# One-hot rows by wide transpositions and small transfers in the start of a routed attention and SwiGLU kernel

## The chip, the cores and the metric

The kernel runs on one core of one Trainium2 chip. The metric is the device time of one execution in microseconds (us), the median of several runs. The core has five engines that work side by side and meet only at semaphores: TensorE (PE, with weight loads shown apart as PEld), VectorE (DVE), ScalarE (ACT), GpSimd (POOL) and SyncE (SP, which here only issues transfers). Each engine runs its own instructions in the order in which they were written.

## The reference

Attention in which a query sees only the keys of its own cluster, then a SwiGLU feed-forward layer without biases. There are 4 batches, 8 heads, 768 positions, 64 columns a head, 16 clusters a head; the layer has width 512 and inner width 1536.

```python
q_assign = np.argmax(np.einsum('bhsd,hcd->bhsc', q_n, c_n), axis=-1)
k_assign = np.argmax(np.einsum('bhsd,hcd->bhsc', k_n, c_n), axis=-1)
mask = q_assign[:, :, :, None] == k_assign[:, :, None, :]
scores = np.where(mask, scale * np.matmul(q, k.transpose(0, 1, 3, 2)), -1e9)
attn = exp(scores - max); attn = attn / sum(attn)
x = np.matmul(attn, v)                      # then (tokens, 512)
xn = x / sqrt(mean(x * x) + 1e-6) * rms_g
out = (silu(xn @ w_gate) * (xn @ w_val)) @ w_out
```

## The kernel before, in words

**The mask as sixteen more rows.** For each head the transposed queries and keys are kept in bf16 tiles `qext` and `kext`, 80 rows high: 64 rows of the head and below them 16 rows that hold, for each position, a one-hot of its cluster. The matmul over 80 rows (L349, `s`) then gives the score plus a large constant where the clusters agree, and the exponential on ACT (L353, `pT`) takes the constant off again, so that pairs of different clusters vanish. Everything below about `kext` and `qext` is about filling these two parts in time: the 64 rows by casts (L241), the 16 rows by the one-hot path.

**Units and steps.** A unit is half of a batch's queries (384 positions) with all 8 heads. A head of a unit is three steps; each step is two score matmuls (L349) into one of two PSUM buffers and one exponential of 128 x 768 (L353). `attention` writes the steps out in order and puts other work between them. I number the 24 steps of the first unit 0 to 23; head h has steps 3h to 3h + 2. The steps after them belong to the second unit. After the middle step of each head it issues `pv` of the head before: 18 matmuls (L367, `acc`) that multiply the exponentials with the values. Two heads share one `acc` tile, and there is only one buffer for it (`ps_a`); after the odd head DVE takes the reciprocal of the sums (L372, `inv`) and scales (L374, `x`), which frees the buffer for the next two heads. So pv of heads 2, 4 and 6 waits for an x. This pv is written right after a step's scores, and the next step's scores stand behind it on PE.

**The first unit has no feed-forward work to fill it.** From the second unit on, matmuls of the feed-forward layer for the unit before stand between the scores. The first unit's gaps instead hold the preparation of the eight heads of batch 0, written out by hand in `first`, a table from step to function, with `gap1` and `gap5` for steps 1 and 5. Steps that have no entry get one warming matmul (`more`, L133); those with `None` get nothing.

**Preparation of a head.** Queries and keys are loaded by SP, turned by PE in three 128 x 128 transposes (`trans`, L222, tile `tq` in PSUM), and copied to `qkT` by ACT (L228) or by DVE (L226). POOL casts `qkT` into `kext` and `qext` (`casts`, L241); a head needs its two halves of keys (K0, K1) and the first half of queries (Q0) for the first unit, and Q1 for the second. POOL also casts the values (`vcast`, L244) and issues the loads of the gate and value weights (`load_gv`, L205). Group 0 is heads 0 to 3, group 1 heads 4 to 7; `trans(1, h, m)` is head 4 + h, keys for m = 1, queries for m = 0. `late` is the same for the first heads of batch 1.

**The one-hot path before.** `pair_clusters(p)` serves heads 2p and 2p + 1: PE multiplies `qkT` with the centroids (L321, `sc`), then DVE transposes (L324), takes the largest of 16 (L327) and compares (L328), which writes zeros and ones into `pads[p]`: 128 partitions, 32 for each of two heads and queries or keys. `head(n)` then calls `under` twice: one DVE transposition of 32 x 384 (L333) writes the keys' 16 rows, and the padding below them, straight into `kext`, another the queries' into `qext`. The rows go through DVE in 32-bit words that hold two bf16 values.

**Order before.** Step 1: pair_clusters(1), then heads 4 to 7's preparation begins, head(2), head(3). Step 5: pair_clusters(2), head(4). Step 7: head(5). Step 9: pair_clusters(3). Step 10: head(6). Step 13: DVE casts head 6's keys itself, then head(7). Step 14 issues second_batch, loads for batch 1, behind `hold`, a small transfer by SP that waits for an inv. At the second unit's step 5 the first unit's normalized tokens are transposed (L429), and then the first gate matmul (L450) runs. `norm` before it is a chain on DVE: squares (L392), a root (L403, L145 to L154), scaling (L414).

Of the kernel before, what the change touches and what calls it, by code (L numbers as in the profile page):

```python
# [10 lines left out]
BF16 = mybir.dt.bfloat16  # L11
I32 = mybir.dt.int32
# [10 lines left out]
def kernel(  # L23
# [12 lines left out]
    nc = tc.nc  # L36
    B, H, S, D = q.shape
    NC = centroids.shape[1]
# [6 lines left out]
    HG = 4  # L45
# [52 lines left out]
    def load_qk(n):  # L98
        if n < B * H:
            load(n, 0)  # L100
            load(n, 1)
# [22 lines left out]
    qext = [const.tile([P, HG, S], BF16, name=f"qext{i}") for i in range(4)]  # L124
    kext = [const.tile([P, HG, S], BF16, name=f"kext{i}") for i in range(4)]
# [76 lines left out]
    def load_gv(i):  # L202
        c = slice(i * DF // 2, (i + 1) * DF // 2)
        for w, of in ((wg, moe_w_gate), (wv, moe_w_val)):
            nc.gpsimd.dma_start(out=w[:, :, c], in_=of[:, c].rearrange("(c p) f -> p c f", p=P))  # L205
# [7 lines left out]
    def trans(g, h, part, on=None):  # L213
        if (g, h // 2) not in qkT:
            qkT[g, h // 2] = qk32.tile([P, 2, 2, UQ], F32, tag="qkT", name="qkT")
        qk = staged[g * HG + h]
        if g * HG + h >= BH:
            nc.vector.transpose(qkT[g, h // 2][:, h % 2, part], qk[:, part].rearrange("p t d -> p (t d)"))  # L218
            return
        ps = ps_g.tile([P, UQ], F32, tag="gen", name="tq")  # L220
        for i in range(HT):
            nc.tensor.transpose(ps[:, i * P:(i + 1) * P], qk[:, part, 2 * i:2 * i + 2].rearrange("p t d -> p (t d)"),  # L222
                                ident_f)
        to, by = qkT[g, h // 2][:, h % 2, part], 1.0 / ZS if part and g < BG else 1.0
        if on is nc.vector:
            nc.vector.tensor_scalar_mul(to, ps, by)  # L226
        else:
            nc.scalar.activation(to, ps, ACT.Copy, scale=by)  # L228
# [5 lines left out]
    def cast(on, g, h, part, es=(0, 1)):  # L234
        for e in es:
            to = cols((kext if part else qext)[g % 4][:D, h], g, e)
            of = qkT[g, h // 2][e * D:(e + 1) * D, h % 2, part]
            if on is nc.scalar:
                nc.scalar.copy(to, of)
            else:  # L240
                on.tensor_copy(to, of)  # L241

    def vcast(n):
        nc.gpsimd.tensor_copy(vbf[n // HG % 4][:, n % HG, :, :D], stagedv[n])  # L244
# [48 lines left out]
    def place(on, g, m, es=(0, 1)):  # L293

        ext = (kext if m else qext)[g % 4]
        for h in range(HG):
# [7 lines left out]
    pads = [(xp if p == 0 else outp).tile([P, NB, 32, 2], BF16, tag="o_sb" if p else "gvT", name=f"pads{p}")  # L304
            for p in range(H // 2)]
# [3 lines left out]
    def slot(n, m):  # L309

        return 32 * (2 * (n % 2) + m if n < 2 else 2 * m + n % 2)

    def pair_clusters(p, heads=(0, 1)):
        g, h = divmod(2 * p, HG)
        what = [(h + i, m) for i in heads for m in range(2)]
        at = [slot(2 * p + i, m) for i in heads for m in range(2)]
        r = slice(min(at), max(at) + 32)
        pool, tag = (ps_g, "gen") if p else (ps_s, "s") if 0 in heads else (ps_a, "acc")
        ps = pool.tile([P, 512], F32, tag=tag, name="sc")
        for a, (hh, m) in sorted(zip(at, what)):  # L320
            nc.tensor.matmul(ps[a:a + 32, :UQ], lhsT=cblk[:, g * HG + hh], rhs=qkT[g, hh // 2][:, hh % 2, m],  # L321
                             start=True, stop=True)
        sct = asg.tile([P, UQ], F32, tag="scT", name="scT", bufs=2)
        nc.vector.transpose(sct[r], ps[r, :UQ])  # L324
        cl = sct[r].rearrange("p (b e c) -> p b e c", e=2, c=NC)
        mx = ps[r, UQ:UQ + 2 * NB].rearrange("p (b e) -> p b e", e=2)
        nc.vector.tensor_reduce(mx, cl, axis=AX, op=ALU.max)  # L327
        nc.vector.tensor_tensor(pads[p][r, :, :NC].rearrange("p b c e -> p b e c"), cl,  # L328
                                mx.unsqueeze(3).broadcast_to([mx.shape[0], NB, 2, NC]), op=ALU.is_equal)

    def under(n, m):
        i = slot(n, m)
        nc.vector.transpose((kext if m else qext)[n // HG][D:D + 32, n % HG].bitcast(I32),  # L333
                            pads[n // 2][i:i + 32].rearrange("p b c e -> p (b c e)").bitcast(I32))
# [239 lines left out]
    def tokens(g, h, on=None):  # L574
        trans(g, h, 1, on)
        trans(g, h, 0, on)

    def head(n):
        under(n, 1)
        under(n, 0)  # L580

    def casts(on, n, *what):
        for m, e in what:
            cast(on, n // HG, n % HG, m, (e,))

    K0, K1, Q0, Q1 = (1, 0), (1, 1), (0, 0), (0, 1)
    pool_ = nc.gpsimd
# [31 lines left out]
    def more():  # L619
        busy(1, False)  # L620
# [3 lines left out]
    def second_batch():  # L624
        nc.sync.dma_start(out=hold, in_=invs[0].rearrange("p a t -> p (a t)"))
        for n in range(H + HG, H + NQ):
            load_qk(n)
        for n in range(H, H + AV):
            load_v(n)
        nc.sync.dma_start(out=grow, in_=moe_rms_g.unsqueeze(0).broadcast_to([P, DM]))  # L630

    def gap1():
        pair_clusters(1)
        tokens(1, 1)
        casts(pool_, 2, Q1)
        casts(pool_, 3, Q1)
        vcast(2)
        vcast(3)
        head(2)
        head(3)  # L640
        casts(pool_, 4, K0, K1, Q0)
        load_gv(0)
        casts(pool_, 5, K0, K1, Q0)

    def gap5():
        pair_clusters(2)
        casts(pool_, 6, Q0)
        vcast(4)
        casts(pool_, 7, Q0)
        for n in (4, 5):  # L650
            casts(pool_, n, Q1)
        vcast(5)
        casts(pool_, 7, K0, K1)
        vcast(6)
        vcast(7)
        for n in (6, 7):
            casts(pool_, n, Q1)
        load_gv(1)
        head(4)

    early = [lambda h=h, m=m: trans(1, h, m) for h in (2, 3) for m in (1, 0)]
    late = [lambda h=h, m=m: trans(2, h, m, nc.vector if h < 3 else None) for h in range(HG) for m in (1, 0)]
    first = {0: lambda: trans(1, 0, 0), 1: gap1, 2: early[0], 3: early[1], 4: lambda: (early[2](), early[3]()), 5: gap5,
             7: lambda: head(5), 9: lambda: pair_clusters(3), 10: lambda: head(6),
             13: lambda: (casts(nc.vector, 6, K0, K1), head(7)), 14: lambda: (more(), second_batch())}
    first.update({16: None, 19: None, 22: None})
    first.update({i: f for i, f in zip((15, 17, 18, 20, 21, 23), late)})


    due = []  # L670
# [22 lines left out]
    for u in range(1, NU):  # L693
        ffn, o, g = ffn_work(u - 1), out_work(u - 2) if u > 1 else [], u + 2
        if u == 1:
            ffn[:2] = [(2 * 0.64, lambda: gv_first(0)), (0.0, lambda: None)]
            t, c, a = group_work(2)
            t3, c3, a3 = group_work(3)
            n = LEAD - 4
            w3 = weave(t3[n:], c3)  # L700
            prep = c + a + w3[:4] + [(0.0, lambda: load_o(8))] + w3[4:] + a3[:5]
            idle = const.tile([P, 1], BF16)

            def norm():
                rms(0)
                nc.gpsimd.tensor_copy(idle, xn[0][:, CC - 1, HT - 1, P - 1:])
                for h in range(HG):
                    casts(pool_, H + h, K0, Q0, K1, Q1)

            hooks = {(1, 0, 0): late[6], (1, 0, 1): lambda: (late[7](), norm())}  # L710
            hooks.update({(1, *divmod(2 + i, HT)): t3[i][1] for i in range(n)})
            hooks[1, *divmod(LEAD - 1, HT)] = lambda: xtrans_all(0)
            fill = spread(ffn[:CUT], prep)
            attention([(1, h) for h in range(H)], fill, LEAD, hooks)
        else:
            fill = ffn_work(u - 2)[CUT:]
            fill = fill[:1] + spread(fill[1:], [(0.0, f) for _, f in (a3[5:] if u == 2 else rest)])
            fill.append((0.0, lambda u=u: rms(u - 1)))
            rows, clusters = group(g)
            fill += [(0.0, lambda n=n: load_qk(n)) for n in LATE.get(u, ())]  # L720
            n, m = {2: (8, 4), 3: (12, 4)}.get(u, (len(rows), len(clusters)))
            fill += spread(o, rows[:n]) + spread(ffn[:CUT], [(0.0, f) for _, f in rows[n:]] + clusters[:m])
            rest = clusters[m:]
            attention([(u, h) for h in range(H)], fill, 1 if g < NG else 0, ahead=1)
# [42 lines left out]
```

The softmax here doesn't subtract the row's maximum and nothing guards it: scores larger than these inputs give would overflow.

## Time and profile before

| | |
|---|---|
| time, median of 3 runs | 325.4 us (325.24 to 325.67) |
| span of the profiled execution | 323.6 us |
| PE busy | 317.5 us, 98% |
| ACT busy | 245.0 us, 76% |
| DVE busy | 217.7 us, 67% |
| POOL busy | 134.0 us, 41% |
| exponential of one step (L353) | 904 ns, 192 of them |
| cast to kext or qext by POOL (L241) | 540 and 532 ns |
| transposition of 128 x 384 by DVE (L218) | 552 ns |

A line of the page names line of code, engine, operation, output and input, and then either the start and length of one merged stretch or count, sum and mean. "Idle before" names what released the engine. A busy PE is not PE at its peak, since the ends of matmuls are modelled, and shares over the whole span hide that the stages differ: the first 40 us, in which the first unit runs without feed-forward work, have another limit than the rest.

### The profile page before, as it was taken

How to read it: one execution, taken by the hardware profiler on the slowest of the kernel's cores; microseconds unless marked ns; L12 is line 12 of the kernel's file. 1: busy time of each engine (PE TensorE's matmuls, PEld its weight loads, DVE VectorE, ACT ScalarE, POOL GpSimd, SP SyncE). 2: the span in 40 equal slices, each digit the busy share in tenths (PEclk: the TensorE clock that was granted, in tenths of full speed). 3: DMA queues.
4: the chain of work that ended last, by engine and by line, in shares of the span. 5: the costliest groups of instructions: out<-in, count | busy, mean ns of one | idle time of the engine just before them, and what ended most of it. 6: DMA issues, size and time to landing. Idle time of an engine off the chain costs nothing.

```text
span 323.6 us, 7771 instructions
## 1 busy us (share of the span) xinstructions
PE 317.5 (98%) x2847; PEld 190.4 (59%) x2847; DVE 217.7 (67%) x502; ACT 245.0 (76%) x422; POOL 134.0 (41%) x275
## 2 busy tenths in 40 slices
PE   8999999999999999999999999999999999999996
PEld 4546656565656656565566655665566656654654
DVE  6999879888586857779677685876265645681430
ACT  5999988986869877787679867897879868862322
POOL 5998198978933585046917156440000000000000
PEclk9999999999999999999999999999999999999999
DMA  7999985998445664565456440000500040004002
GB/s 254 339 234 219 200 212 100 176 172 186 80 72 118 154 130 74 117 134 139 82 93 133 134 115 34 9 18 1 149 0 2 2 113 34 0 2 138 11 1 98
DMA packets 91639, 34.64 MB, mean 107 GB/s; under 512 B 75600, under 2 KB 88528, under 8 KB 91600
## 3 DMA queue, kind: packets, MB, share of 16 engines
q1 hardware_dynamic: 84544, 27.84, 36.7%
q0 software_dynamic: 6768, 5.90, 10.3%
q8 instruction: 22, 0.36, 0.5%
q10 hardware_dynamic: 288, 0.39, 0.4%
q14 instruction: 17, 0.14, 0.1%
HBM read 28.61 MB, written 6.29 MB: 108 GB/s over the span
## 4 chain that ended last, share of the span: by engine, by line
PE 86%; ACT 4%; POOL 4%; DVE 3%; issue 1%; DMA 1%; ACTq 0%; DVEq 0%; POOLq 0%
PE gate L450 19%; PE val L450 19%; PE o L488 18%; PE s L349 17%; PE acc L367 9%; ACT pT L353 3%; PE sc L255 3%; POOL kext L241 2%; POOL qext L241 1%; DMA boot<-in_centroids_dram 1%; PE o L499 1%; POOL vbf L244 1%; ACT qkT L228 1%; DVE kext L333 1%; DVE qext L333 1%
## 5 line engine op out<-in xcount | busy, mean ns | idle before, releaser
L353 ACT ACTIVATE pT<-s,off 128x768 bf16<-128x768 f32 x192 | 170.9, 904 | 29.1 <-PE s L349 28.3
L349 PE MATMUL s<-qext,kext 80*128 80x384 bf16 x384 | 94.8, 327 | 1.2 <-ACT pT L353 0.6
L450 PE MATMUL gate<-xnT,wg 128*128 128x384 bf16 x384 | 78.6, 325 | 0.1
L450 PE MATMUL val<-xnT,wv 128*128 128x384 bf16 x384 | 78.4, 326 | 0.0
L488 PE MATMUL o<-wo,gvT 128*128 128x512 bf16 x276 | 67.7, 378 | 0.0
L472 DVE SCALAR_TENSOR_TENSOR th<-th,gate 128x384 f32<-128x384 f32 x81 | 44.5, 549 | 34.1 <-ACT th L471 33.7
L349 PEld LDWEIGHTS <-kext 80*128 80x128 bf16 x384 | 36.3, 98 | 35.0 <-issue 7.6
L476 DVE SCALAR_TENSOR_TENSOR gvT<-th,val 128x384 bf16<-128x384 f32 x81 | 44.4, 548 | 8.5 <-PE val L450 2.9
L450 PEld LDWEIGHTS <-wg 128*128 128x128 bf16 x384 | 36.2, 97 | 23.4 <-issue 0.3
L471 ACT ACTIVATE th<-gate 128x384 f32<-128x384 f32 x81 | 39.7, 490 | 12.6 <-PE gate L450 11.8
L367 PEld LDWEIGHTS <-pT 128*128 128x128 bf16 x1152 | 43.4, 97 | 9.8 <-DVE x L374 0.8
L450 PEld LDWEIGHTS <-wv 128*128 128x128 bf16 x384 | 35.7, 97 | 22.4 <-issue 0.4
L367 PE MATMUL acc<-vbf,pT 128*128 128x65 bf16 x1152 | 45.6, 193 | 0.5 <-DVE x L374 0.2
L488 PEld LDWEIGHTS <-gvT 128*128 128x128 bf16 x276 | 25.9, 97 | 26.1 <-issue 0.2
L241 POOL CAST qext<-qkT 64x384 bf16<-64x384 f32 x64 | 33.7, 532 | 17.1 <-DVE qkT L218 9.6
L298 POOL DMA_DIRECT2D qext<-oh x48 | 23.1, 492 | 34.9 <-DVE oh L287 34.9
L241 POOL CAST kext<-qkT 64x384 bf16<-64x384 f32 x60 | 32.4, 540 | 5.1 <-DVE qkT L226 2.4
L298 POOL DMA_DIRECT2D kext<-oh x48 | 23.1, 488 | 13.6 <-DVE oh L287 12.5
L491 ACT COPY o_sb<-o 128x512 f32<-128x512 f32 x23 | 13.5, 585 | 17.6 <-PE o L488 17.6
L372 DVE RECIPROCAL inv<-acc 128x6 f32<-128x6 f32 x32 | 6.0, 188 | 24.9 <-PE acc L367 24.4
L218 DVE STREAM_TRANSPOSE qkT<-qk 128x384 f32<-128x384 f32 x38 | 19.5, 552 | 0.0
L374 DVE TENSOR_TENSOR x<-acc,inv 128x384 f32<-128x384 f32 x32 | 17.8, 557 | 1.1
(80 smaller groups left out, 220.6 us busy)
## 6 DMA issues: line engine op xcount, KB each, us to landing
vs<-in_v_dram SPq DMA_DIRECT2D x32, 192.0 KB, 4.1
out_dram<-o_sb SPq DMA_DIRECT2D x23, 256.0 KB, 2.5
qk<-in_q_dram SPq DMA_DIRECT2D x76, 48.0 KB, 2.7
qk<-in_k_dram SPq DMA_DIRECT2D x76, 48.0 KB, 2.5
qk<-in_q_dram SPq DMA_DIRECT2D x13, 192.0 KB, 4.8
qk<-in_k_dram SPq DMA_DIRECT2D x11, 192.0 KB, 4.9
wg<-in_moe_w_gate_dram POOLq DMA_DIRECT2D x2, 768.0 KB, 7.9
wv<-in_moe_w_val_dram POOLq DMA_DIRECT2D x2, 768.0 KB, 11.8
```

The lines of the kernel that those rows point to most:

```text
L218: nc.vector.transpose(qkT[g, h // 2][:, h % 2, part], qk[:, part].rearrange("p t d -> p (t d)"))
L241: on.tensor_copy(to, of)
L298: on.dma_start(out=ext[D:D + NC, h, e * UQ:(e + 1) * UQ], in_=put[g, m][32 * h + e * NC:32 * h + (e + 1) * NC])
L349: nc.tensor.matmul(ps[:, j, :w] if nt == HT else flat[:, j * w:(j + 1) * w], lhsT=cols(kext[g % 4][:KR, hh], g, kc // HT, kc % HT * P, (kc ...
L353: nc.scalar.activation(pT[u, h][:, n * i:n * i + n, :w], of, ACT.Exp, bias=off, scale=scale if g >= BG else scale * ZS)
L367: nc.tensor.matmul(acc[:, h % 2, t], lhsT=pT[u, h][:, kc, t * P:(t + 1) * P], rhs=vbf[g % 4][:, hh, kc % HT * 2 + kc // HT], start=kc == 0 ...
L374: nc.vector.tensor_tensor(dst, acc[:, :, :nt, :D], inv[:, :, :nt].unsqueeze(3).broadcast_to([P, 2, nt, D]), op=ALU.mult)
L450: nc.tensor.matmul(ps, lhsT=(wv if val else wg)[:, c, f * P:(f + 1) * P], rhs=xnT[u][:, c], start=c == 0, stop=c == CC - 1)
L471: nc.scalar.activation(th, ps, ACT.Tanh, scale=0.5)
L472: nc.vector.scalar_tensor_tensor(th, th, 1.0, ps, op0=ALU.add, op1=ALU.mult)
L476: nc.vector.scalar_tensor_tensor(gvT[u][:, f, :n], gates[u], 0.5, ps, op0=ALU.mult, op1=ALU.mult)
L488: nc.tensor.matmul(outs[u], lhsT=gvT[u][:, f, t * P:(t + 1) * P], rhs=wo[:, f], start=f == 0, stop=f == FC - 1)
```

## The change

It shortens DVE's and ACT's work in the first unit. For heads 5, 6 and 7 the narrow transpositions into `kext` and `qext` go. In their place one transposition of all 128 partitions of `pads[p]` (`send`) writes the rows to the `scT` tile that pair_clusters has just finished with, and small transfers on SP's queue, two for each head, carry 16 rows each to their place: two for head 5, four for heads 6 and 7. pair_clusters(3) moves from step 9 to step 7 so that the transfers start early. Head 6's key casts go from DVE to POOL, whose list is put into a new order, and vcast(4) moves ahead of the weight load. Three copies from PSUM (L228 by ACT) become L226 by DVE: head 5's queries at step 1, head 7's queries at step 4, and one of the late ones. The late transposes start one step earlier, at step 14.

```diff
+        rows[p] = sct.bitcast(I32)
+
+    rows = {}
+
+    def send(p, heads):
+
+        nc.vector.transpose(rows[p], pads[p].rearrange("p b c e -> p (b c e)").bitcast(I32))
+        for n in heads:
+            for m in (1, 0):
+                i = slot(n, m)
+                nc.sync.dma_start(out=(kext if m else qext)[n // HG][D:D + NC, n % HG], in_=rows[p][i:i + NC].bitcast(BF16))
...
     def gap1():
+        trans(1, 1, 0, nc.vector)
         pair_clusters(1)
-        tokens(1, 1)
+        trans(1, 1, 1)
         casts(pool_, 2, Q1)
         casts(pool_, 3, Q1)
         vcast(2)
...
         casts(pool_, 4, K0, K1, Q0)
+        casts(pool_, 5, K0, K1)
+        vcast(4)
         load_gv(0)
-        casts(pool_, 5, K0, K1, Q0)
+        casts(pool_, 5, Q0)
 
     def gap5():
         pair_clusters(2)
         casts(pool_, 6, Q0)
-        vcast(4)
+        vcast(5)
+        casts(pool_, 6, K0, K1)
         casts(pool_, 7, Q0)
-        for n in (4, 5):
-            casts(pool_, n, Q1)
-        vcast(5)
+        casts(pool_, 4, Q1)
+        vcast(6)
         casts(pool_, 7, K0, K1)
-        vcast(6)
+        casts(pool_, 5, Q1)
         vcast(7)
         for n in (6, 7):
             casts(pool_, n, Q1)
         load_gv(1)
         head(4)
-
-    early = [lambda h=h, m=m: trans(1, h, m) for h in (2, 3) for m in (1, 0)]
-    late = [lambda h=h, m=m: trans(2, h, m, nc.vector if h < 3 else None) for h in range(HG) for m in (1, 0)]
+        send(2, (5,))
+
+    def gap7():
+        pair_clusters(3)
+        send(3, (6, 7))
+
+    early = [lambda h=h, m=m: trans(1, h, m, nc.vector if (h, m) == (3, 0) else None) for h in (2, 3) for m in (1, 0)]
+    late = [lambda h=h, m=m: trans(2, h, m, nc.vector if (h, m) != (HG - 1, 0) else None) for h in range(HG) for m in (1, 0)]
     first = {0: lambda: trans(1, 0, 0), 1: gap1, 2: early[0], 3: early[1], 4: lambda: (early[2](), early[3]()), 5: gap5,
-             7: lambda: head(5), 9: lambda: pair_clusters(3), 10: lambda: head(6),
-             13: lambda: (casts(nc.vector, 6, K0, K1), head(7)), 14: lambda: (more(), second_batch())}
+             7: gap7, 14: lambda: (late[0](), second_batch())}
     first.update({16: None, 19: None, 22: None})
-    first.update({i: f for i, f in zip((15, 17, 18, 20, 21, 23), late)})
+    first.update({i: f for i, f in zip((15, 17, 18, 20, 21, 23), late[1:])})
...
-            hooks = {(1, 0, 0): late[6], (1, 0, 1): lambda: (late[7](), norm())}
+            hooks = {(1, 0, 0): late[7], (1, 0, 1): norm}
```

Steps 9, 10 and 13, which lose their entries, get a warming matmul each; step 14 loses its own.

## The prediction

> **What bounds the kernel now.** I read the slices of the page first, then the chain that ended last, then the busy time by stretch, then the timeline of each engine between 10 and 41 us. From 40 us on TensorE (PE) is at 9 tenths in every slice and the chain is nothing but PE. All the edits act before that, so the question is when the first gate matmul starts, at 40.21 us before; what moves it should move the end by as much, since the PE-bound stretch behind it keeps its work.
>
> Busy time by stretch (PE, weight loads, DVE, ACT, POOL; count of instructions in brackets):
>
> ```profile
> 17.80:22.20 4.40, 4.12 (x51) 1.96 (x48) 3.97 (x9) 4.17 (x7) 4.22 (x8) 1.00 0.91 225
> 22.20:28.20 6.00, 5.62 (x73) 3.42 (x70) 5.58 (x11) 5.75 (x8) 5.71 (x11) 1.00 1.07 188
> 28.20:34.50 6.30, 6.12 (x85) 4.75 (x84) 6.12 (x17) 6.30 (x8) 3.38 (x6) 1.00 1.11 206
> 34.50:40.20 5.70, 5.16 (x55) 3.76 (x54) 4.67 (x22) 5.38 (x10) 0.68 (x3) 1.00 1.28 214
> ```
>
> No one engine is far ahead: DVE and ACT are both near full until 34.5 us, POOL until 28. So the order of work on DVE decides as much as its sum. The chain says where it decides (start, length, what):
>
> ```profile
> 19.87 0.57 DVE kext L333
> 20.46 0.57 DVE qext L333
> 21.06 0.21 DVE inv L372
> 21.29 0.56 DVE x L374
> 21.88 0.57 DVE kext L333
> 22.48 0.57 DVE qext L333
> 23.08 0.59 DVE scT L324
> ...
> 26.47 0.57 DVE x L374
> 27.08 0.72 PE acc L367 x18
> ```
>
> Seven microseconds of the chain are DVE, and it leaves DVE at an x (L374), the instruction that frees the one accumulator bank. The timeline shows the same at the x before it:
>
> ```profile
> 21.29 0.56 DVE L374 TENSOR_TENSOR x<-acc,inv 128x384 f32<-128x384 f32 x1
> ...
> 21.93 0.71 PE L367 MATMUL acc<-vbf,pT 128*128 128x65 bf16 x18
> 22.13 2.58 ACT L353 ACTIVATE pT<-s,off 128x768 bf16<-128x768 f32 x3 [0.23 <-PE s L349]
> ...
> 22.48 0.51 PE L349 MATMUL s<-qext,kext 80*128 80x384 bf16 x2
> ...
> 28.19 6.46 ACT L353 ACTIVATE pT<-s,off 128x768 bf16<-128x768 f32 x8 [0.25 <-PE s L349]
> ```
>
> x ends at 21.85, PE starts head 2's acc matmuls at 21.93, and step 11's scores (22.48) stand behind them. ACT's exps run 0.80 us apart with idle gaps of only 0.2 us.
>
> **What the Trainium skill says.** "TensorE: Matmul & The Clock Gate", section on the 16 sub-arrays, says that ScalarE's and VectorE's queues are strict first-in first-out: work that can wait, put ahead of an x, delays it by its whole length. The timeline agrees: DVE ran its 0.57 us transpositions ahead of the reciprocal although pv(0, 1) was done by about 19.8. "DMA: Bandwidth & Descriptors", section on the anatomy of one DMA, prices any transfer at about 2.0 us fixed; the small one-hot transfers of later groups (L298) land here in 2.5 us (kext) and 3.1 us (qext), median. The same page, section on queues, rings and completion order, says that an engine serves the rows in turn, a packet of 9 to 17 descriptors at a time. This trace has one small transfer from SP amid a weight load, and it is slow:
>
> ```profile
> q0 software_dynamic: 702, 1.05, 116.2%
> ...
> hold<-inv SPq DMA_DIRECT2D x1, 3.0 KB, 5.6
> ```
>
> hold took 5.6 us from issue to landing. The first line is the weights' queue from 23.5 to 28.5 us: 702 records in 16 engines x 5 us x 1.162, so 0.13 us each, and a turn of 9 to 17 costs 1.2 to 2.2 us (an estimate).
>
> **The change, part by part.** Steps are the 24 scores of the first unit.
>
> ACT copies. Three of L228 go to DVE. A copy between two exps stretches their distance from 0.80 to 1.16 us (36.51 to 37.66), so 0.37 each, 1.1 in all; two fall before step 5, one after 34.5. The first gains almost nothing at once: step 2's scores on PE end at 13.64 and its exp began at 13.76. The second brings exp 5 from 17.79 to about 17.2. Then PE stands in the way: the cluster products of heads 4 and 5 (0.78) still precede step 6's scores (17.76), and those of heads 6 and 7 move from behind step 9 to behind step 7 and its acc matmuls: 0.34 + 0.55 + 0.78 = 1.67 us between two scores where ACT needs 0.80. Exp 8 comes at about 20.5 instead of 20.2 and exp 10 at about 22.1, as before (22.13). So ACT's gain is spent by step 10.
>
> DVE before the first x. In the changed kernel's order of instructions there is added ahead of it: two copies (L226; three took 1.49 us, 0.47 from one to the next; I take 0.5) and the transposition of all of pads2, 128x384. That is not in the trace as such; the nearest row is L218, 128x384 in 552 ns, and transpositions follow each other at 0.60, so 0.60. In sum 1.6 us (1.5 to 1.7). Nothing ahead of the x is removed: head 5's two narrow transpositions stood behind it. So the reciprocal goes from 21.06 to 22.66, x ends at 23.45, and pv(0, 2) starts at 23.5 instead of 21.93. PE waits there some 1.7 us, and behind it stand its 18 matmuls (0.55), one warm matmul that now replaces head(6) at step 10 (0.22, from 0.17 for 384 columns), and step 11's scores: 24.27. From scores to exp took 0.46, so exp 11 is at 24.73 instead of 22.94: +1.79 us.
>
> DVE after it. Six narrow transpositions less one wide one (heads 5, 6, 7; the other wide one is counted above), and head 6's two casts: 6 x 0.60 - 0.60 + 1.26 = 4.3 us less. It shortens nothing but the wait at pv(0, 4): the second x is no longer last, and the idle before exp 17 (0.25, with its tail about 0.3) goes. From exp 11 ACT sets the pace, so exp 23 ends later by 1.79 - 0.3 = 1.5.
>
> The tail. From exp 23 (33.84) to the first gate matmul (40.21) the chain is pv, x, squares, root and xn on DVE, 6.4 us that no edit touches. ACT ran beside it, and with one copy fewer the xn transposes no longer wait for step 29's scores: 0.15 to 0.2 back. Sum so far: +1.3 us.
>
> POOL gets head 6's two key casts (2 x 0.64). Its work ends near 33.5 instead of 31.6, and POOL was idle from there to 39.3: hidden. The weight loads are issued about 2 us later (21.75 and 32): needed only at 40 and near 58 us.
>
> The transfers. Head 5's two follow the first wide transposition (22.0 to 22.6) and are issued at 22.7 and 23.2; 3.1 us later is 26.3, and step 15's scores want them when exp 13 ends, 24.73 + 2 x 0.80 + 0.90 = 27.2: hidden. Those of heads 6 and 7 follow the second wide transposition: scT 23.5, maximum 24.2, comparison 24.8, transposition 25.5 to 26.0; k6 issued at 26.1, q6 at 26.5. Step 18's scores are due when exp 16 ends, 24.73 + 5 x 0.80 + 0.90 = 29.7. At 2.5 us q6 lands at 29.0 and costs nothing; at hold's 5.6 it lands at 32.1 and costs 2.4. The first weight load runs just then. I take one turn of waiting, 1.7 us, on top of 2.5: 30.7, a stall of 1.0. On SP, head 8's later loads queue behind and have time. Head 7 (wanted at about 33) is in time.
>
> Sum: 325.4 + 1.3 + 1.0 = 327.7 us.
>
> **The rivals.**
> - Transfers hidden: only the late x counts. For it: L298's 2.5 us; one row of 1,536 bytes per partition is little. Against: hold's 5.6. Time 325.4 + 1.3 = 326.7.
> - Transfers wait out the weight load. Issued 2 us later than before (19.76), its records would end near 32 instead of 29.9; with 0.9 to completion q6 lands near 32.8, a stall of 3.1: 329.8. For it: hold had to wait almost to the load's end. Against: the skill's turns.
> - Faster: DVE gives the x in time because my sum ahead of it is wrong, so ACT keeps its three copies (1.1) and the two idle gaps (0.5): 323.8. For it: DVE's total falls by 2 us or more (-4.3 + 1.6 + the late copy 0.5), and the chain runs through DVE. Against: in that order x stands behind the added work.
> - Break-even: the late x costs 0.5 less, ACT's lead 0.5 more, transfers hidden: 325.5.
>
> **How the numbers follow.** Late x and a transfer stall of about 1: 0.37, 327.7. Late x alone: 0.30, 326.7. Waiting out the load: 0.10. Break-even: 0.10. Faster: 0.13. Slower by over 0.2% (326.05) is 0.37 + 0.30 + 0.10 = 0.77. The range, 325.2 to 329.2, holds the first two, most of break-even and the shorter of the long stalls, 0.79 in all, and leaves out faster and the longest.
>
> **What would show it.** Right: x of heads 0 and 1 ends near 23.4, PE idle before pv(0, 2) released by it for over 1 us, ACT idle about 1.7 us before exp 11, then exps without gaps to a wait of step 18 on the kext or qext transfers; first gate matmul near 42.5. Wrong: x ends before 22.3, exp 11 before 23.5, or a first gate matmul under 40.2. If step 18 shows no wait, the transfers were priced too high; if step 15 shows one, too low.

## The result, and the profile after

The changed kernel takes 328.54 us (median of 6 runs, 327.85 to 329.55) where the kernel before took 325.38 in the same comparison. The ratio is 1.0098, with a 95% interval of 1.0080 to 1.0116: about 3.2 us slower. The prediction said 327.7, range 325.2 to 329.2. The ratios in this document leave out disturbed executions, some per cent longer at a lower granted clock; the times are medians of all executions, and where disturbed ones move the median by much, only the ratio is given. Lines of code after the change are 11 higher than before it from L333 on (scores L360, exponentials L364, acc L378, x L385, gate L461); the narrow transpositions are L344, the wide ones L336, the transfers L340.

The first gate matmul starts at 42.95 us instead of 40.21. From there to the reciprocal of the last attention unit the two traces run in parallel, 2.74 us apart (288.11 against 285.37), as the stretch that TensorE bounds should. What is to be explained lies before 43 us. The busy time of the changed kernel in the four stretches that the prediction showed (PE, weight loads, DVE, ACT, POOL, then clock, DMA share and GB/s):

```profile
17.80:22.20 4.40, 4.19 (x47) 1.94 (x39) 4.16 (x9) 3.69 (x6) 4.16 (x9) 1.00 0.48 148
22.20:28.20 6.00, 4.29 (x53) 2.57 (x51) 4.55 (x10) 4.63 (x6) 5.77 (x10) 1.00 0.86 124
28.20:34.50 6.30, 5.58 (x66) 4.37 (x67) 3.13 (x8) 5.05 (x8) 4.84 (x9) 1.00 1.18 240
34.50:40.20 5.70, 5.11 (x62) 3.81 (x62) 4.77 (x22) 5.39 (x9) 0.00 (x0) 1.00 1.25 209
```

In the second and third row DVE falls from 5.58 and 6.12 us to 4.55 and 3.13. The work was taken off DVE as intended. But PE and ACT fall too, ACT from 5.75 and 6.30 to 4.63 and 5.05: the engine that sets the pace now waits. The timeline of DVE, PE and ACT shows two places (start, length, instruction, and in brackets the idle time before it with what ended it):

```profile
22.15 0.58 DVE L336 STREAM_TRANSPOSE scT<-pads 128x384 int32<-128x384 int32 x1
...
22.85 0.56 DVE L385 TENSOR_TENSOR x<-acc,inv 128x384 f32<-128x384 f32 x1
...
23.46 0.72 PE L378 MATMUL acc<-vbf,pT 128*128 128x65 bf16 x18 [0.97 <-DVE x L385]
...
24.78 3.49 ACT L364 ACTIVATE pT<-s,off 128x768 bf16<-128x768 f32 x4 [1.26 <-PE s L360]
...
28.92 0.50 PE L360 MATMUL s<-qext,kext 80*128 80x384 bf16 x2 [1.25 <-POOL kext L241]
...
29.52 8.04 ACT L364 ACTIVATE pT<-s,off 128x768 bf16<-128x768 f32 x10 [1.25 <-PE s L360]
```

The first is the late x: it ends at 23.41, PE waits 0.97 us for it, and exp 11 starts at 24.78. The second is at step 15: four exponentials, 11 to 14, stand in one stretch, and then there is a gap of 1.25 us. The profile puts that wait down to a cast by POOL. But the matmul waits for several semaphores, and the profile names only the event that came last: POOL's cast of that moment is head 7's keys, while head 5's casts, which step 15 reads, had been written by 24.1. The chain of waits follows the same wrong arrow:

```profile
27.78 0.51 POOL vbf L244
28.29 0.55 POOL kext L241
28.84 0.08 issue
28.92 0.51 PE s L360 x2
```

What else step 15 waits for is head 5's two transfers. SP issues them here:

```profile
22.76 0.63 SPq L340 DMA_DIRECT2D kext<-scT  x1
23.44 0.58 SPq L340 DMA_DIRECT2D qext<-scT  x1
```

and the list of transfers issued between 22 and 24.5 us gives their size and the time from issue to landing:

```profile
kext<-scT SPq DMA_DIRECT2D x1, 24.0 KB, 5.7
qext<-scT SPq DMA_DIRECT2D x1, 24.0 KB, 5.3
```

23.44 + 5.3 is 28.74, and the scores start at 28.92. POOL issued the first weight load at 21.90 and 22.80, so both transfers lived beside it. Those of heads 6 and 7, issued at 25.75 to 27.56, took 4.7 to 5.7 us. Head 6's had landed by 31.0, and step 18's scores ran at 31.27 without a wait, because step 15 had delayed everything by then; without that delay they would have been due near 30.0 and would have waited about 1.1 us (an estimate from these times).

The traces do not start at one clock: exp 0, ahead of all edits, is at 11.07 before and 11.39 after, and between 10.99 and 11.68 in the experiments. Counted from exp 0 the gate matmul moved by 2.42 us. Exp 11 came 1.44 later (before, it starts at 23.02). Exp 14 lost another 0.22, where the warming matmul that fills step 13 now stands between pv and the scores; experiment 1, which has none there, lacks this loss. Exp 15 lost 1.30. Of this, 0.37 came back at exp 17, whose idle gap is gone, and 0.17 in the tail.

### The profile page after: what moved, and what is told of

It is laid out like the page before. It is cut to its first block, busy times and chain, and to the rows that moved or that the text cites. A ratio compares the mean times of both kernels' runs of the same rounds, so it can differ in the third digit from the quotient of the medians.

```text
span 326.9 us, 7768 instructions
## 1 busy us (share of the span) xinstructions
PE 317.4 (97%) x2835; PEld 191.4 (59%) x2849; DVE 215.7 (66%) x499; ACT 244.1 (75%) x419; POOL 135.2 (41%) x277
## 4 chain that ended last, share of the span: by engine, by line
PE 85%; ACT 6%; POOL 5%; DVE 1%; issue 1%; DMA 1%; ACTq 0%; POOLq 0%
PE gate L461 19%; PE val L461 18%; PE o L499 18%; PE s L360 17%; PE acc L378 9%; ACT pT L364 4%; PE sc L255 3%; POOL kext L241 2%; POOL qext L241 2%; DMA boot<-in_centroids_dram 1%; PE o L510 1%; ACT qkT L228 1%; POOL vbf L244 0%; ACT xn L405 0%; DVE x L385 0%
## 5 line engine op out<-in xcount | busy, mean ns | idle before, releaser
L364 ACT ACTIVATE pT<-s,off 128x768 bf16<-128x768 f32 x192 | 170.9, 903 | 31.9 <-PE s L360 31.1
L360 PE MATMUL s<-qext,kext 80*128 80x384 bf16 x384 | 94.7, 327 | 2.4 <-POOL kext L241 1.3
L461 PE MATMUL gate<-xnT,wg 128*128 128x384 bf16 x384 | 78.6, 325 | 0.1
L461 PE MATMUL val<-xnT,wv 128*128 128x384 bf16 x384 | 78.4, 326 | 0.0
L483 DVE SCALAR_TENSOR_TENSOR th<-th,gate 128x384 f32<-128x384 f32 x81 | 44.5, 550 | 34.2 <-ACT th L482 33.8
L499 PE MATMUL o<-wo,gvT 128*128 128x512 bf16 x262 | 66.0, 378 | 0.8
L360 PEld LDWEIGHTS <-kext 80*128 80x128 bf16 x384 | 36.5, 98 | 36.1 <-issue 6.7
L461 PEld LDWEIGHTS <-wg 128*128 128x128 bf16 x384 | 36.2, 97 | 23.6 <-issue 0.6
L378 PEld LDWEIGHTS <-pT 128*128 128x128 bf16 x1152 | 43.5, 97 | 10.3 <-DVE x L385 1.4
L461 PEld LDWEIGHTS <-wv 128*128 128x128 bf16 x384 | 35.7, 97 | 22.4 <-issue 0.4
L378 PE MATMUL acc<-vbf,pT 128*128 128x65 bf16 x1152 | 45.7, 193 | 1.1 <-DVE x L385 1.0
L241 POOL CAST qext<-qkT 64x384 bf16<-64x384 f32 x64 | 33.8, 534 | 18.0 <-DVE qkT L218 9.6
L241 POOL CAST kext<-qkT 64x384 bf16<-64x384 f32 x62 | 33.6, 541 | 4.6 <-DVE qkT L226 2.4
L385 DVE TENSOR_TENSOR x<-acc,inv 128x384 f32<-128x384 f32 x32 | 17.8, 558 | 1.1
```

The lines of the kernel that those rows point to most:

```text
L360: nc.tensor.matmul(ps[:, j, :w] if nt == HT else flat[:, j * w:(j + 1) * w], lhsT=cols(kext[g % 4][:KR, hh], g, kc // HT, kc % HT * P, (kc ...
L364: nc.scalar.activation(pT[u, h][:, n * i:n * i + n, :w], of, ACT.Exp, bias=off, scale=scale if g >= BG else scale * ZS)
L378: nc.tensor.matmul(acc[:, h % 2, t], lhsT=pT[u, h][:, kc, t * P:(t + 1) * P], rhs=vbf[g % 4][:, hh, kc % HT * 2 + kc // HT], start=kc == 0 ...
L385: nc.vector.tensor_tensor(dst, acc[:, :, :nt, :D], inv[:, :, :nt].unsqueeze(3).broadcast_to([P, 2, nt, D]), op=ALU.mult)
L461: nc.tensor.matmul(ps, lhsT=(wv if val else wg)[:, c, f * P:(f + 1) * P], rhs=xnT[u][:, c], start=c == 0, stop=c == CC - 1)
L483: nc.vector.scalar_tensor_tensor(th, th, 1.0, ps, op0=ALU.add, op1=ALU.mult)
```

## The experiments

Unless said otherwise, each starts from the changed kernel.

**1. No transfers.** The one-hots of heads 5, 6 and 7 by narrow transpositions in their old steps.

```diff
-        send(2, (5,))
-             7: gap7, 14: lambda: (late[0](), second_batch())}
+             7: lambda: head(5), 9: lambda: pair_clusters(3), 10: lambda: head(6), 13: lambda: head(7),
+             14: lambda: (late[0](), second_batch())}
```

> The changed kernel with the one-hots of heads 5, 6, 7 by narrow transpositions again, in their old steps (7, 9, 10, 13); the two early copies by VectorE and the casts by GpSimd stay. My theory is that the loss of 3.2 us is a late first x (1.6 us of added VectorE work ahead of it: two copies 1.0, the wide transposition 0.6) and a wait of 1.25 us in step 15 for head 5's transfers. Then here x of heads 0, 1 ends at 22.8 (23.41 in the changed kernel), exp 11 begins near 24.1 (24.78), step 15 shows no wait, and the time is 326.4 to 326.9, about 1.9 us less than the changed kernel and still 1 to 1.5 more than before. Rival: the copies by VectorE are what costs, and the transfers little; then the time stays above 327.8.

Measured: 325.88 us, ratio 1.0016 (1.0009 to 1.0023). In the timeline of this kernel the late x is still there, the wait of step 15 is not (six exponentials, 11 to 16, in one stretch):

```profile
21.99 0.56 DVE L385 TENSOR_TENSOR x<-acc,inv 128x384 f32<-128x384 f32 x1
...
22.60 0.72 PE L378 MATMUL acc<-vbf,pT 128*128 128x65 bf16 x18 [0.89 <-DVE x L385]
...
23.70 4.92 ACT L364 ACTIVATE pT<-s,off 128x768 bf16<-128x768 f32 x6 [1.05 <-PE s L360]
```

So wide transpositions, transfers and the earlier step of pair_clusters(3) that goes with them cost 2.66 us of the 3.2 together, more than I expected, and the rest of the change about 0.5. The earlier step was not tested alone. From exp 0 to the end of x it is 11.56 here, 12.02 in the changed kernel and 10.78 before: the wide transposition ahead of x is worth 0.46, the two copies 0.78.

**2. The two early copies by ACT again.**

```diff
-        trans(1, 1, 0, nc.vector)
+        trans(1, 1, 0)
-    early = [lambda h=h, m=m: trans(1, h, m, nc.vector if (h, m) == (3, 0) else None) for h in (2, 3) for m in (1, 0)]
+    early = [lambda h=h, m=m: trans(1, h, m) for h in (2, 3) for m in (1, 0)]
```

> The changed kernel with the two early copies (head 5's queries in step 1, head 7's queries in step 4) by ScalarE again; wide transpositions, transfers and casts stay. Theory: x of heads 0, 1 ends 1.0 earlier, 22.4, and exp 11 begins near 23.8; the transfers of head 5 are issued 1.0 earlier too (21.8 and 22.4), so the wait of step 15 stays between 0.6 and 1.3. Time 327.5, 1.0 less. Rival: ScalarE sets the pace in steps 1 to 10, two copies of 0.37 come back to it, and the time stays within 0.3 of 328.5.

Measured: 328.21 us, ratio 1.0089 (1.0063 to 1.0114), which cannot be told from the changed kernel's time. Yet x came 0.77 earlier counted from exp 0, and behind step 8, whose gap of 0.7 to 0.8 both kernels have, ACT's timeline shows no gap until step 15, where PE waited 1.50 us. The list of transfers issued from 21.5 to 23 us says why:

```profile
kext<-scT SPq DMA_DIRECT2D x1, 24.0 KB, 1.9
qext<-scT SPq DMA_DIRECT2D x1, 24.0 KB, 5.6
```

Both move 24 KB on one queue. The keys' was issued at 21.68 and landed in 1.9 us; the queries' was issued 0.68 later and took 5.6, to 27.96 (step 15's scores: 28.13). Between them POOL's weight load got going. My theory gave this edit 1.0 us. Counted from exp 0, exp 11 came 0.74 earlier than in the changed kernel, exp 15 0.48 and the first gate matmul 0.43: the late transfer took about a third of the gain back, and what was left is too small for these runs to tell. The rival's time came true, its reason only in part: with two copies back on ACT exp 8 came 0.4 later, but the wait for x absorbed that.

**3. The first weight load later**, five lines (six casts) down POOL's list.

```diff
-        load_gv(0)
...
         casts(pool_, 7, Q0)
+        load_gv(0)
```

> The changed kernel with the first load of the gate and value weights issued by GpSimd five casts later, near 26 instead of 21.9 us; all else stays. Theory: the transfers of head 5 took 5.3 to 5.7 us because the weight load fills the DMA engines; without it they land in 2.5 to 3.5 us, by 26.7, step 15 shows no wait and the time is 1.2 less, 327.3. Heads 6 and 7 are issued at 25.8 to 27.6, mostly ahead of the load's first records, so no wait moves to step 18. Rival: about 5 us is what such a transfer costs with or without a load beside it; then they land at 28.5 as before, step 15 waits 1.2 us and the time stays at 328.5.

Measured: ratio 1.0198 (1.0138 to 1.0257). The profiled execution took 337.1 us, longer than that ratio stands for, so the argument rests on its first 35 us alone. Head 5's transfers, issued at 23.04 and 23.71, met no load:

```profile
kext<-scT SPq DMA_DIRECT2D x1, 24.0 KB, 1.9
qext<-scT SPq DMA_DIRECT2D x1, 24.0 KB, 1.9
```

and step 15 did not wait. So about 5 us is no fixed price; the load makes it. But the load, now issued at 25.58, took the next ones: head 6's queries (issued at 26.57) needed 5.4 us and step 18 waited 1.74 us. I had written that no wait would move there. The rest of the loss lies later, and why is open, since no typical trace of it was taken. Part of it is a lower clock: the other three executions have a mean granted clock of 0.995, the changed kernel 0.998 to 1.000. In the profiled one TensorE waited 4.63 us up to 69.04, at cluster products of a later batch, and the clock fell to 0.50 from 68.0 on.

**4. x ahead of the wide transposition.** The line `send(2, (5,))` moves from the end of gap5 to the head of gap7.

```diff
         head(4)
-        send(2, (5,))
     def gap7():
+        send(2, (5,))
         pair_clusters(3)
```

> The changed kernel with the wide transposition of heads 4 and 5 and its two transfers moved from the end of step 5's list to the head of step 7's, so that x of heads 0, 1 stands ahead of it on VectorE. Theory: x ends 0.6 earlier, 22.8, and exp 11 begins at 24.2, but head 5's transfers are issued some 0.6 later and land near 29.3, so step 15 waits 2.4 to 2.5 instead of 1.25: from step 15 on everything is 0.6 later, time 328.9 to 329.2. Rival: the late x alone sets the end and step 15's wait is slack that other work would take anyway; then the time falls by 0.6 to 327.9.

Measured: 331.11 us, ratio 1.0174 (1.0144 to 1.0203). The two moves are as expected: PE waits 0.52 instead of 0.97 us for x, and 2.37 us at step 15.

```profile
29.20 0.80 PE L360 MATMUL s<-qext,kext 80*128 80x384 bf16 x2 [2.37 <-POOL kext L241]
```

But the time is 2 us above my 329. The busy times by stretch show what else happened (the third column from the end is the granted clock):

```profile
24.00:28.00 4.00, 2.62 (x30) 1.57 (x28) 2.57 (x6) 3.32 (x4) 3.77 (x8) 1.00 1.08 191
28.00:32.00 4.00, 2.81 (x24) 2.15 (x25) 0.56 (x1) 1.59 (x2) 3.81 (x7) 0.60 1.18 223
32.00:36.00 4.00, 4.00 (x36) 2.99 (x34) 1.11 (x2) 2.51 (x4) 0.81 (x2) 0.55 1.17 236
36.00:40.00 4.00, 3.82 (x51) 2.88 (x48) 3.63 (x11) 3.88 (x6) 0.00 (x0) 1.00 1.27 211
```

TensorE ran at half its clock for 6.8 us. The table's stretches of 4 us blur this: cut into halves of a microsecond, the column reads 0.79 from 28.5, 0.50 in every stretch from 29.0 to 35.5, and 0.89 from 35.5.

**5. The same with TensorE kept busy**: six matmuls that compute nothing in step 14.

```diff
-             7: gap7, 14: lambda: (late[0](), second_batch())}
+             7: gap7, 14: lambda: (late[0](), busy(6, False), second_batch())}
```

> The kernel with head 5's transfers sent behind x, plus six warming matmuls (128 x 512 each, about 0.22 us) behind step 14's scores, which fill most of the 2.4 us that TensorE waits for head 5's one-hots. They compute nothing. Theory: that kernel took 331.1 instead of 329.0 because the granted clock fell to 0.55 to 0.60 for some 8 us after the wait; with TensorE kept at work the wait it shows is near 1.1 us, the clock stays at 1.00 from 28 to 36 us, and the time is 328.9 to 329.3 though the transfers land no earlier. Rival: the clock fell for another reason, or the warming delays step 15 itself; then the time stays at 331 or rises.

Measured: 329.07 us, ratio 1.0129 (1.0104 to 1.0155). PE's wait at step 15 shows as 0.94 us, now put down to the transfer itself, and the clock stays at 1.00:

```profile
29.37 0.50 PE L360 MATMUL s<-qext,kext 80*128 80x384 bf16 x2 [0.94 <-DMA qext<-scT]
```

Work without any use saves 2.0 us by the medians and 1.5 by the ratios, whose intervals touch. So the drop of the clock was the cost beyond the wait itself, and it came from TensorE standing idle.

**6. Only heads 6 and 7 by transfers.** Head 5 narrow in step 7.

```diff
-        send(2, (5,))
     def gap7():
+        head(5)
         pair_clusters(3)
```

> The changed kernel with head 5 alone by narrow transpositions (in step 7, behind x of heads 0, 1 and ahead of the cluster work of heads 6, 7); heads 6 and 7 keep the wide transposition and the transfers. Theory: removing the wait of step 15 only uncovers one in step 18. Exp 11 begins some 0.5 earlier than in the changed kernel and step 15 has no wait, so step 18 is due near 29.0; the second wide transposition comes 0.6 to 0.7 later, head 6's transfers are issued at 26.4 and 27.0 beside the weight load and land near 31.5 to 32, so step 18 waits 2 to 3 us, and the time is 328.0 to 329.0, no gain. Rival: head 5's two transfers are the whole loss; then the time falls to the 325.9 of the kernel with all three heads narrow.

Measured: 333.21 us, ratio 1.0239 (1.0218 to 1.0261). The direction is as my theory had it, the size is not: head 6's transfers (issued at 26.38 and 27.05) took 6.9 and 6.4 us, to 33.45; step 18 waited 4.29 us, and the clock fell to 0.50 from 32.8 us on, again for 6.8 us.

**7. Head 5's transfers first.** Two lines of gap5 swapped.

```diff
-        head(4)
         send(2, (5,))
+        head(4)
```

> The changed kernel with two lines of step 5's list swapped: the wide transposition of heads 4 and 5 and its transfers stand ahead of head 4's narrow transpositions, so the transfers are issued about 1.2 us earlier, near 21.6 and 22.2, before the weight load's first records (23.5); x of heads 0, 1 and the load stay where they are. Theory: records of the load are what makes a transfer slow, so both of head 5's land about 2 us after their issue, by 24.5, and step 15's wait of 1.25 us goes; step 18 is then due at 29.7, head 6's transfers land at 31.0 as before, and step 18 waits 1.0 to 1.4 in its place: time 328.2 to 328.8, no gain. Rival: the transfers of heads 6 and 7 are harmless, or come earlier on a queue that the first two don't hold up; then 327.3.

Measured: 332.65 us, ratio 1.0219 (1.0206 to 1.0233). Transfers issued from 22 to 23.5 us and in flight then:

```profile
kext<-scT SPq DMA_DIRECT2D x1, 24.0 KB, 1.9
qext<-scT SPq DMA_DIRECT2D x1, 24.0 KB, 3.8
```

They landed by 26.0 and step 15's wait is gone, with POOL's casts where they were: it was the transfers. Then step 18 waits instead:

```profile
33.55 0.80 PE L360 MATMUL s<-qext,kext 80*128 80x384 bf16 x2 [3.37 <-DMA qext<-scT]
```

Head 6's queries, issued at 26.42, took 7.0 us where the same transfer had taken 4.7. I had expected 31.0 for its landing and it was 33.4; the clock fell again (0.50 from 32.0 us on, for 6.8 us). In the changed kernel step 15's wait had hidden some 1.1 us of such a wait. Why the transfer landed 2.4 us later here, with the load issued at the same time (21.89), is not shown.

**8. Without transfers and without early copies.** Experiment 1 with the copies of experiment 2; what is left are head 6's casts on POOL, POOL's order and the late copy.

```diff
-        trans(1, 1, 0, nc.vector)
+        trans(1, 1, 0)
-    early = [lambda h=h, m=m: trans(1, h, m, nc.vector if (h, m) == (3, 0) else None) for h in (2, 3) for m in (1, 0)]
+    early = [lambda h=h, m=m: trans(1, h, m) for h in (2, 3) for m in (1, 0)]
```

> The changed kernel without any transfer and without the two early copies by VectorE: heads 5, 6, 7 narrow in their old steps, ScalarE copies as before; what is left of the change is head 6's key casts by GpSimd, GpSimd's new order and one late copy by VectorE. Theory: the 0.5 us that the kernel with all three heads narrow still lost against the kernel before was the late x (0.8 us), so without the copies x ends at the old distance from exp 0, the second x comes at least 0.2 earlier, ScalarE has one copy less: 324.8 to 325.2, 0.2 to 0.6 better than before. Rival: the copies paid for themselves by ScalarE's 0.7 us and the rest of the change costs; then the time is 325.9 or more.

Measured: 325.17 us, ratio 1.0003 (0.9985 to 1.0021). So the early copies cost 0.7 us by the medians (325.88 less 325.17) and by the first gate matmul, which came 0.71 earlier after exp 0 than in experiment 1; by the ratios it is 0.4, and their intervals overlap. What is left is neither gain nor loss. My 0.2 to 0.6 was wrong: the second x comes at 26.47 as before, since head 6's casts on DVE had stood behind it, not ahead.

**9. Both x first.** Experiment 1 with head 5's query copy by ACT, head 4's narrow transpositions behind the first x and head 6's behind the second.

```diff
-        trans(1, 1, 0, nc.vector)
+        trans(1, 1, 0)
...
-        head(4)
...
-             7: lambda: head(5), 9: lambda: pair_clusters(3), 10: lambda: head(6), 13: lambda: head(7),
+             7: lambda: (head(4), head(5)), 9: lambda: pair_clusters(3), 13: lambda: (head(6), head(7)),
```

> The kernel without transfers and with head 5's query copy by ScalarE again, and VectorE's list put in the order in which things are due: head 4's narrow transpositions move from step 5 to step 7, behind x of heads 0, 1, and head 6's from step 10 to step 13, behind x of heads 2, 3; head 7's query copy stays with VectorE. Theory: the order on VectorE ahead of an x is what costs. x of heads 0, 1 ends about 0.7 earlier than before, the second x about 1 earlier, both idle gaps of ScalarE (0.23 and 0.25) go and it has two copies less (0.7): 324.2 to 324.8. Rival: the gaps were slack, or heads 4 and 6 now come late for steps 12 and 18; then 325.3 or more.

Measured: 325.25 us, ratio 1.0002 (0.9994 to 1.0010). No gain, though both x came over 1 us earlier (20.26 and 25.22 instead of 21.29 and 26.47). The gaps moved on; the timeline of ACT:

```profile
21.84 0.90 ACT L364 ACTIVATE pT<-s,off 128x768 bf16<-128x768 f32 x1 [0.23 <-PE s L360]
22.95 6.50 ACT L364 ACTIVATE pT<-s,off 128x768 bf16<-128x768 f32 x8 [0.21 <-PE s L360]
29.74 4.96 ACT L364 ACTIVATE pT<-s,off 128x768 bf16<-128x768 f32 x6 [0.29 <-PE s L360]
```

None of the three comes from an x. The first is the cluster products that PE runs in step 9, the second the warming matmul that fills step 10 once head 6 has left it, the third late transposes that wait for a PSUM buffer whose copy stands behind head 7's transpositions on DVE.

**10. The work behind those three gaps moved**, from experiment 9.

```diff
-             7: lambda: (head(4), head(5)), 9: lambda: pair_clusters(3), 13: lambda: (head(6), head(7)),
+             7: lambda: (head(4), head(5)), 8: lambda: pair_clusters(3), 10: None, 13: lambda: head(6),
...
-    first.update({16: None, 19: None, 22: None})
+    first.update({16: lambda: head(7), 19: None, 22: None})
```

> The narrow kernel with both x first on VectorE, put further into the order of due times: the cluster products of heads 6 and 7 in step 8 in place of a warming matmul (step 9 before), no warming matmul in step 10, head 7's narrow transpositions in step 16, behind two of the late copies. In the kernel with x first three idle gaps of ScalarE were left, 0.23 before exp 10 (products in step 9), 0.21 before exp 11 (the warming matmul that took head 6's place in step 10) and 0.29 before exp 19 (late transposes that wait for copies behind head 7's transpositions on VectorE). Theory: ScalarE's exponentials, 0.80 us apart, are the bound of this stretch, and each gap that goes moves the first gate matmul by as much: 324.3 to 324.8, 0.5 to 1.0 better than before. Rival: the gaps move on to later steps or the tail behind exp 23 takes them; then 325.0 or more.

Measured: ratio 1.0000 (0.9984 to 1.0016). Two of the gaps are closed; that of the cluster products stands one step earlier (0.32 us before exp 9), and behind it sixteen exponentials ran without a gap. The first gate matmul came 28.33 us after exp 0, 0.81 earlier than before: the expected gain, in full, at 40 us. At 84 us of this trace it is gone:

```profile
84.21 0.81 PE L461 MATMUL gate<-xnT,wg 128*128 128x384 bf16 x4 [0.97 <-DMA xnT<-xn]
```

SyncE's queue shows why. Its loads for batch 1 kept it until 78.18 (75.33 before), and the transfer that transposes the second unit's tokens stands behind them:

```profile
75.27 2.91 SPq L107 DMA_DIRECT2D vs<-in_v_dram  x4
78.36 1.44 SPq L428 DMA_TRANSPOSE xnT<-xn  x1
```

**11. POOL's order nearly as before**, from experiment 10: the weight loads are issued at 19.98 and 30.00 instead of near 21.6 and 31.5.

```diff
-        casts(pool_, 5, K0, K1)
-        vcast(4)
         load_gv(0)
-        casts(pool_, 5, Q0)
+        casts(pool_, 5, K0, K1, Q0)
...
+        vcast(6)
+        load_gv(1)
         vcast(7)
         for n in (6, 7):
             casts(pool_, n, Q1)
-        load_gv(1)
```

> The kernel in the order of due times, with GpSimd's list near its order before the change: the first load of the gate and value weights ahead of head 5's casts again (19.8 instead of 21.6), the second ahead of the last casts (near 30 instead of 31.5); head 6's key casts stay with GpSimd. In the kernel in the order of due times the first gate matmul came 0.8 us earlier counted from exp 0, but later SyncE issued its loads until 78.2, so the transposition of the second unit's normalized tokens behind them was issued 1.0 later than in the kernel before and TensorE waited 0.97 us for it at 84.2. Theory: the transfers of batch 1, not the engines, take the gain back, and the weight loads ahead of them set their pace; with the loads 1.5 to 1.8 us earlier the wait at 84 us goes and the time is 324.3 to 324.9. Rival: the transfers are full in any case and the wait stays; then 325.0 to 325.7, no difference from before.

Measured: 324.86 us, ratio 0.9976 (0.9965 to 0.9987): faster than the kernel before by 0.4 us by the medians and 0.8 by the ratio, and than the changed one by some 3.7 to 4. The transposing transfer is issued at 77.09 and PE does not wait for it. Experiment 10's interval rests on three executions and overlaps with this one, so it is the traces, not the times, that show the wait gone.

Of the 0.81 us at the gate 0.32 were left here (28.82 from exp 0). The traces show where the rest went. In experiment 10 POOL's last cast ended at 31.8, just after the first of DVE's squares of 128 x 384 (L403) had begun at 31.55; here the last casts stand behind the second load and ran beside these squares until 33.8. Two of these squares took 0.91 and 0.90 us instead of 0.58 and 0.55, one cast 1.03 instead of about 0.5, and the x behind them came 0.48 later after exp 0. That the two engines held each other up is likely, but was not tested.

## Why the prediction was right, point by point

**The bound.** Right for all but 0.5 us: 2.42 us arise before the first gate matmul and are carried to the end. A further 0.5 us stands at the very end, most of it from the end of SP's last issue to the end of the span: 2.2 us before, 2.6 after. It goes with the transfers, far earlier though they are: 2.2 us in all six kernels without them, 2.4 to 2.9 in all seven with them. Why is open.

**ACT's copies.** Right that their gain is spent by step 10: with cluster products in step 7, exp 8 waits 0.71 us, and exp 10 starts about 11.2 us after exp 0 against 11.1 before, with two copies fewer on ACT. Experiment 8 prices the two copies at a loss of 0.4 to 0.7 us.

**The late x.** The mechanism was right, and the end of x (23.41, predicted 23.45) agreed by luck of the traces' start. The term of 1.6 us measured 1.24: 0.78 for the two copies (predicted 1.0) and 0.46 for the wide transposition (predicted 0.60). Exp 11 came 1.44 later, predicted 1.79. The prediction knew of the warming matmul in step 10, but not of the 0.22 that the one in step 13 costs.

**The second x, and the tail.** Right: 0.3 predicted and 0.37 measured at exp 17, 0.15 to 0.2 predicted and 0.17 measured in the tail. (The 33.84 in the prediction is the end of exp 23, not its start.)

**Transfers.** This is the step that failed, though its sum held. The prediction priced head 5's transfers at 3.1 us, from transfers later in the kernel that meet no weight load, called them hidden, and charged the load's turn to heads 6 and 7 alone, as a stall of 1.0 in step 18. In the trace head 5's took 5.7 and 5.3 us and step 15 stalled 1.25; the load had been issued just ahead of them, as the prediction itself says (21.75). The sum held by luck: the stall at step 15 replaced the one at step 18, whose size the prediction had nearly right (1.0, against some 1.1 that were hidden), so the gate moved by 2.42 us where 2.3 were forecast, and with the 0.5 at the end, which was not forecast, the time was still inside the range.

The prediction took the 2.0 us of "DMA: Bandwidth & Descriptors", section on the anatomy of one DMA, as the price of any transfer, while the section gives it for GpSimd's path. On SP's queue experiments 2, 3 and 7 show both prices of one transfer: 1.9 us without records of the load, 3.8 to 7.0 with them. For heads 6 and 7 the predicted 4.2 (1.7 on 2.5) was too small: 4.7 to 5.7 in the changed kernel, 4.6 to 7.0 in experiments 6 and 7. Whether 327.7 would have come out had head 5's landed in time is doubtful: experiment 7 comes closest to that case, and it took 332.65. Waiting out the load (32.8), given one chance in ten, was the better picture of head 6's landing there (33.4), though not in the changed kernel (31.0, where 30.7 was forecast).

**The rivals.** "Transfers hidden" and "break-even" fall with step 15's wait, which experiment 7 traces to the transfers. "Faster" falls with the order on DVE: x stood behind the added work. None of them knew of the clock.

**POOL.** Right that its longer list costs nothing up to the gate. That its weight loads come 2 us later was called harmless because the weights are needed only at 40 and 58 us; the traces of experiments 10 and 11 show that it is not once the front is faster, since other loads queue behind.

## What to carry to other kernels

Moving work from a full engine to the DMA engines changes a fixed cost into one that depends on what else is in flight: before a small transfer is put on a path with a due time, list the large transfers issued within its lifetime and price it beside them, from the slowest small transfer that the trace has. Look first at where the full engine's work stands, not at how much there is: here putting the narrow work in order brought the first gate matmul forward by 0.81 us (experiment 10), and removing it put the matmul back by 2.42. And a gain at the front can be lost again in a queue behind it, that of the loads too, which does not come forward with it.

## What the runs showed of the hardware

A transfer of 24 KB between two tiles took 1.9 us alone and 3.8 to 7.0 us beside a load of weights by POOL's queue (36 transfers in seven traces, median 5.4); two of one queue, issued 0.68 us apart, took 1.9 and 5.6. The Trainium skill, "DMA: Bandwidth & Descriptors", section on queues, rings and completion order, has an engine take its rings in turn by packets; the one turn of 1.2 to 2.2 us that the prediction worked out from it is too little: beside the load the delays were 1.9 to 5.1 us, over 2.7 in 34 of the 36.

Waits of TensorE of 2.37, 3.37 and 4.29 us brought its granted clock to 0.50, each time for 6.8 us, while waits of 1.25, 1.50 and 1.74 us left it at 1.00. The skill's "TensorE: Matmul & The Clock Gate", part on the clock gate, puts the drop at an idle window of about 3.4 us. Here a single wait of 2.37 us was enough, well short of that figure: the clock fell at 28.8 us, when TensorE had been idle for only 2.0, and then stayed low through 6.4 us of nearly full work. Such a drop cost 1.5 to 2 us beyond the wait itself (experiments 4 and 5: 331.11 against 329.07). It seems not to last equally long in every execution: of the four in experiment 4, two have a mean granted clock of 0.988 and took 331.7 and 331.9 us, two have 0.994 and 0.995 and took 330.5 and 330.4.
